# Spectral mix with a gated MLP: the first MLP block as seven products, with the first two products of three blocks ahead of the rest

## The chip, the cores and the metric

The kernel runs on one core of a Trainium2 chip. The time is device microseconds of one execution; three runs of the kernel before gave a median of 782.64 us (781.74 to 783.07). The core's engines work from queues of their own and wait for one another through semaphores: PE (TensorE, matrix multiply), DVE (VectorE), ACT (ScalarE), POOL (GpSimd) and SP (SyncE). SP and POOL issue nearly all DMAs here.

## The reference, cut to what matters

```python
x = A_x                                                    # 1 x 2048 x 512
g = sigmoid((x * gate_w).sum(-1, keepdims=True))
# FNet mixing: real part of a DFT over the hidden axis, then over the sequence
a = einsum("bsd,ed->bse", x, dft_hid_re)
b = einsum("bsd,ed->bse", x, dft_hid_im)
y = einsum("ts,bse->bte", dft_seq_re, a) - einsum("ts,bse->bte", dft_seq_im, b)
# gated MLP, F = 1792
gate = einsum("bsd,df->bsf", x, W_gate)
up = einsum("bsd,df->bsf", x, W_up)
h = gate * (gate > 0) * up
mlp = einsum("bsf,fd->bsd", h, W_down)
out = g * y + (1 - g) * mlp
```

## The kernel before, in words

All values are float32. Before a matmul each operand is split in two: `hi`, its value rounded to the matmul's input type (a cast), and `lo`, what is left (a subtraction on DVE). A product of two operands is then three matmuls, lo x hi, hi x lo and hi x hi (`PARTS`, L431), summed in PSUM. A cast and a subtraction stand behind every operand, so ACT and DVE feed PE.

Matrix products are made of 2 x 2 blocks, and nearly all of them with seven block products in place of eight, after Strassen and Winograd: some operands are sums of blocks (`x_sum`, `Weights.sum`), and the seven results are combined in PSUM by copying one bank's content into another before the next product is added on top ("seed" in `Block.evac`). The products are numbered 1 to 7 and run in the order 1, 5, 6, 2, 7, 3, 4 (`ORDER`, L25). Products 1 and 2 use the raw blocks of x and of the weights. Products 5, 6, 7, 3 and 4 use sums, or come after them.

The MLP's first stage (`Block`, L539) goes over blocks (c, q): c is one of seven pairs of 128-column groups of W_gate and W_up, and q one of two halves of the tokens. One product of a block is 12 matmuls of 128x512: two outputs i (gate, up), two halves k of the contraction and three parts. So a block of seven products takes 84 matmuls. One block is made otherwise: the first one, (0, 0), with eight plain products (`Direct`, L593), 96 matmuls, from weights laid out a second time in memory (`wf`). It loads x block 11 and its weights in small pieces, so that PE can begin after the first of them. Then come (1, 0), (2, 0), (2, 1), (1, 1) and the others in turn (`sequence`, L1294); block (0, 1) is last, behind the transform over the hidden axis. Behind the MLP's first stage come that transform, the MLP's second stage (`Down`) and the transform over the sequence (`Joint`, `Sequence`). Sums of the DFT matrices that the last stages need are made early, at times when DMA and DVE have room: `right_sums` (L931) loads four 512 KB blocks p, adds them on DVE and stores four sums to memory (`tb`), 18 times, at places from the table `SUMS` (L514).

What sets the order: the text of the kernel only gives each operation a key, which is a place on PE's own path counted in matmuls of 512 columns (0.2267 us each; called a number below). A planner in the kernel (`Plan`, L170) then plays the engines through with fixed costs for each kind of instruction, puts the operations of DVE and ACT in order of due time, and writes out one fixed order for each engine. For DMAs it has a model of its own (`Queues`, L126): a landing 2.4 us after the last byte, and 1.8 us more where another transfer is under way. The keys of prepared operands are in the table `AT` (L512). The weights of later blocks are asked for 66 numbers ahead of their block (`w_prep`, L501; 180 for the last block). Buffers come from 51 units of SBUF, PSUM has eight banks that are taken in turn.

Names in the lists below: `x011` is the loaded x block 11 of token half 0, `x012` and `x022` blocks 12 and 22, `xs5`, `xs6` sums; `xh7`, `xl7` the hi and lo of the x operand of product 7. `wr0`, `wr1` are loaded weights, `wr2`, `wr3` sums of them, `w1h`, `w1l` hi and lo made of `wr1`. In the profile's rows the numbers are left out (`xl`, `wr`), `xb11h` is `Direct`'s hi of x block 11, and `c` is a PSUM bank of the MLP's first stage. All instructions carry L123, the planner's one line of recording, so they are told apart by tile.

Before the first load has landed PE runs eight matmuls on a tile of ones (`warm_up`, L1249), all into one bank.

Of the kernel before, what the change touches and what calls it, by code (L numbers as in the profile page):

```python
# [125 lines left out]
class Queues:  # L126
# [3 lines left out]
    LANDING, BUSY = 2.4, 1.8  # L130
# [211 lines left out]
def kernel(ctx: ExitStack, tc, xP, xG, wf, wgu, wd, cr, ci, wri, gw, out):  # L342
# [129 lines left out]
    class Weights:  # L472
# [6 lines left out]
        def load(self, n):  # L479
            load(self.raw[n].all, wgu[self.c, n])  # L480
# [20 lines left out]
    def w_prep(w, key, ahead=66):  # L501
        for n in range(2):
            op(key - ahead + 6 * n, w.load, n)
        for m, n, k in ((None, 0, -40), (5, None, -36), (6, 2, -30), (7, 1, -12), (3, 3, 0)):
            if m:
                op(key + k, w.sum, m)
            if n is not None:
                op(key + k + 2, w.hi, n)
                op(key + k + 8, w.lo, n)


    AT = {'gate': (66, 52, 482), 'v': (-90, -80, -52, -36, -20, 6, 10, 38, 44), 'lw': (-246, -158, -138, -114, -110, -102), 'll': (-90, 22, 52, 96, 138, 174), 'l0': (-154, -58, -100, -8), 'l1': (-92, -120, -24, 44), 'z': (86,), 'J1': (80, 20, 78, 34, 94), 'J2': (172, 16, 38, 54, 98), 'J3': (136, 24, 56, 60, 64), 'hr': (36, 32, 45), 'rest': (62, 130)}  # L512

    SUMS = {(0, 3, 1): 1520, (0, 1, 1): 210, (1, 2, 0): 2452, (0, 1, 0): 685, (1, 5, 2): 260, (1, 1, 1): 687, (0, 2, 1): 955, (0, 3, 0): 1794, (1, 1, 0): 785, (1, 2, 1): 1000, (0, 2, 0): 377, (1, 4, 0): 444, (1, 3, 0): 655, (1, 3, 1): 800, (1, 5, 3): 1300, (1, 4, 2): 1632, (1, 5, 1): 1045, (1, 5, 0): 541}  # L514
# [24 lines left out]
    class Block:  # L539


        def __init__(self, q, w):
# [4 lines left out]
            for m in ORDER:  # L547
# [3 lines left out]
            h_out(q, w.c, self.h, plan.now + (8 if plan.now > 270 else 100))  # L551
# [11 lines left out]
        def evac(self, m, i):  # L563
# [7 lines left out]
            if m == 1:  # L571
# [19 lines left out]


    class Direct:  # L593
        def __init__(self):
            self.x = {b: [buf(f"xb{b}{x}", dtype=F32R) for x in "hl"] for b in ("11", "21", "12", "22")}

            self.raw = [buf(f"wf{d}", [2, 4, P]) for d in range(2)]
            self.w = [[buf(f"wf{d}{x}", [2, 4, P], F32R) for x in "hl"] for d in range(2)]
            self.g = [buf(f"dg{j}") for j in range(2)]
            self.h = [buf(f"h{d}") for d in range(2)]  # L600
            self.ps = {(f, j): Pair("c") for f in range(2) for j in range(2)}

            for d in range(2):
                for k in range(2):
                    for n in range(3):
                        for i in range(2):
                            pe(2, self.products, [(d, i, f, 0, k, n) for f in range(2)])
                            if d == k == 1 and n == 2:
                                for f in range(2):
                                    op(plan.now, self.evac, f, i, 0)  # L610
            for d in range(2):
                for i in range(2):
                    for f in range(2):
                        pe(6, self.products, [(d, i, f, 1, k, n) for k in range(2) for n in range(3)])
                        if d == 1:
                            op(plan.now, self.evac, f, i, 1)
            h_out(0, 0, self.h, plan.now + 200)
# [10 lines left out]
        def w_load(self, d, k, s=slice(0, 4)):  # L628
            load(self.raw[d][:, k, s], wf[d, :, k, s])

        def w_hi(self, d, k, s=slice(0, 4)):
            E().scalar.copy(self.w[d][0][:, k, s], self.raw[d][:, k, s])

        def w_lo(self, d, k):
            hi, lo = self.w[d]
# [784 lines left out]
```

## Time and profile before

| | us |
|---|---|
| median of three runs | 782.64 |
| profiled execution, its own time | 782.31 |
| its span, first to last instruction | 780.5 |
| PE busy | 774.1 |
| DVE busy | 706.8 |
| ACT busy | 467.4 |
| POOL busy | 119.6 |

The span is 1.8 us shorter than the execution's time; what lies around it is no instruction of the program. Busy time of PE says little about how near it is to its own pace, since matmuls overlap: one takes 389 ns from start to end, and the next starts 227 ns after it. So the distance from one start to the next is what to read, and where it grows PE has waited or its clock was held back.

### The profile page before, as it was taken

How to read it: one execution, taken by the hardware profiler on the slowest of the kernel's cores; microseconds unless marked ns; L12 is line 12 of the kernel's file. 1: busy time of each engine (PE TensorE's matmuls, PEld its weight loads, DVE VectorE, ACT ScalarE, POOL GpSimd, SP SyncE). 2: the span in 40 equal slices, each digit the busy share in tenths (PEclk: the TensorE clock that was granted, in tenths of full speed). 3: DMA queues.
4: the chain of work that ended last, by engine and by line, in shares of the span. 5: the costliest groups of instructions: out<-in, count | busy, mean ns of one | idle time of the engine just before them, and what ended most of it. 6: DMA issues, size and time to landing. Idle time of an engine off the chain costs nothing.

```text
span 780.5 us, 10195 instructions
## 1 busy us (share of the span) xinstructions
PE 774.1 (99%) x3416; PEld 640.3 (82%) x3416; DVE 706.8 (91%) x798; ACT 467.4 (60%) x649; POOL 119.6 (15%) x190
## 2 busy tenths in 40 slices
PE   8999999999999999999999999999999999999997
PEld 6888888888888888888888888888888888888886
DVE  7999898889797978899988579999999999999997
ACT  5654454444444744666565568955648897557672
POOL 0013422232223123212101000001020001010100
PEclk9999999999999999999999999999999999999999
DMA  8446999999989799999999998999989999999991
GB/s 317 181 166 239 381 409 411 379 418 420 418 339 419 303 361 416 418 388 416 376 410 380 406 397 256 371 407 410 309 319 310 375 408 348 335 336 364 314 361 55
DMA packets 78774, 274.12 MB, mean 351 GB/s; under 512 B 8960, under 2 KB 9728, under 8 KB 78720
## 3 DMA queue, kind: packets, MB, share of 16 engines
q1 hardware_dynamic: 52688, 179.47, 60.1%
q0 software_dynamic: 25888, 93.86, 33.6%
q8 instruction: 27, 0.44, 0.2%
q14 instruction: 27, 0.22, 0.1%
q10 hardware_dynamic: 144, 0.13, 0.0%
HBM read 183.76 MB, written 89.66 MB: 350 GB/s over the span
## 4 chain that ended last, share of the span: by engine, by line
PE 97%; DVE 2%; DMA 0%; issue 0%; ACT 0%; SPq 0%; ACTq 0%
PE z L123 39%; PE c L123 35%; PE a L123 10%; PE jB L123 3%; PE jA L123 3%; PE jX L123 2%; PE jD L123 2%; PE jG L123 1%; DVE jcl L123 1%; DVE jo L123 0%; PE jH L123 0%; DMA wf<-wf 0%; DVE jr L123 0%; ACT wf0h L123 0%; DVE wf0l L123 0%
## 5 line engine op out<-in xcount | busy, mean ns | idle before, releaser
L123 PE MATMUL z<-cl,lh 128*128 128x512 f32 x452 | 176.1, 390 | 0.0
L123 PE MATMUL z<-ch,lh 128*128 128x512 f32 x452 | 175.9, 389 | 0.0
L123 PE MATMUL z<-ch,ll 128*128 128x512 f32 x452 | 175.8, 389 | 0.0
L123 DVE TENSOR_TENSOR jcl<-jr,jch 128x1024 fp32r<-128x1024 f32 x84 | 99.5, 1216 | 0.9 <-issue 0.3
L123 PEld LDWEIGHTS z<-cl,lh 128*128 128x128 f32 x452 | 84.8, 188 | 17.9 <-DVE cl L123 0.6
L123 PEld LDWEIGHTS z<-ch,ll 128*128 128x128 f32 x452 | 84.8, 188 | 17.8
L123 PEld LDWEIGHTS z<-ch,lh 128*128 128x128 f32 x452 | 84.8, 188 | 17.7
L123 ACT CAST jch<-jr 128x1024 fp32r<-128x1024 f32 x84 | 85.4, 1053 | 16.8 <-PE z L123 5.8
L123 DVE TENSOR_TENSOR p<-p,p 128x1024 f32<-128x1024 f32 x72 | 86.8, 1219 | 5.6 <-DMA p<-ci 4.9
L123 ACT CAST ch<-r 128x1024 fp32r<-128x1024 f32 x64 | 65.9, 1051 | 36.7 <-DVE r L123 26.3
L123 ACT ACTIVATE c<-c 128x512 f32<-128x512 f32 x78 | 45.4, 583 | 69.0 <-PE c L123 58.1
L123 DVE TENSOR_TENSOR cl<-r,ch 128x1024 fp32r<-128x1024 f32 x64 | 76.9, 1219 | 0.6 <-ACT ch L123 0.4
L123 DVE TENSOR_TENSOR cl<-hr,ch 128x1024 fp32r<-128x1024 f32 (+1 forms) x56 | 60.0, 1087 | 12.7 <-ACT ch L123 8.6
L123 POOL DMA_DIRECT2D tb<-p x72 | 39.3, 546 | 171.6 <-DVE p L123 160.8
L123 ACT CAST ch<-hr 128x1024 fp32r<-128x1024 f32 (+1 forms) x56 | 51.6, 944 | 12.4 <-PE z L123 7.2
L123 PE MATMUL c<-xh,w2l 128*128 128x512 f32 x104 | 40.5, 389 | 0.0
L123 PE MATMUL c<-xl,w2h 128*128 128x512 f32 x104 | 40.5, 389 | 0.0
L123 PE MATMUL c<-xh,w2h 128*128 128x512 f32 x104 | 40.5, 389 | 0.0
L123 PE MATMUL c<-xh,w1l 128*128 128x512 f32 x104 | 40.5, 389 | 0.0
L123 PE MATMUL c<-xl,w1h 128*128 128x512 f32 x104 | 40.5, 389 | 0.0
L123 PE MATMUL c<-xh,w1h 128*128 128x512 f32 x104 | 40.5, 389 | 0.0
L123 ACT COPY a<-a 128x512 f32<-128x512 f32 x40 | 23.1, 579 | 25.9 <-PE a L123 21.0
(229 smaller groups left out, 1636.5 us busy)
## 6 DMA issues: line engine op xcount, KB each, us to landing
tb<-p POOLq DMA_DIRECT2D x72, 512.0 KB, 11.1
p<-ci SPq DMA_DIRECT2D x48, 512.0 KB, 9.3
jr<-tb SPq DMA_DIRECT2D x48, 512.0 KB, 7.7
hr<-hd SPq DMA_DIRECT2D x42, 512.0 KB, 8.6
hd<-hs POOLq DMA_DIRECT2D x28, 512.0 KB, 10.6
ad<-a POOLq DMA_DIRECT2D x28, 512.0 KB, 8.9
p<-cr SPq DMA_DIRECT2D x24, 512.0 KB, 8.4
r<-cr SPq DMA_DIRECT2D x24, 512.0 KB, 12.0
```

What stands on the lines that cost most here:

```text
L123: getattr(getattr(nc, self.engine), self.name)(*map(ap, self.a), **{k: ap(x) for k, x in self.k.items()})
```

## The change

Block (0, 0) is made as the others are, with seven products, and `Direct` and its second copy of the weights are gone. The three blocks c = 0, 1, 2 of token half 0 begin together: product 1 of block 0, product 1 of block 1, product 2 of block 0, product 1 of block 2, product 2 of block 1, product 2 of block 2, half of the contraction after half. The result of product 1 is copied from PSUM to an SBUF buffer `p` by ACT (two copies for each block). Then each block goes on with products 5, 6, 7, 3, 4, after two ACT copies have seeded a bank from `p`.

The first loads are now pieces of the usual weight arrays: x block 11 and the weights of product 1 of blocks 0 and 1, then x block 21 and the weights of product 2. The planner's DMA model adds its 1.8 us only behind its first 10 us. The eight warm-up matmuls go to four banks in turn. The keys of the tables `AT` and `SUMS` are other numbers, among them the places of the sums, where one line shows the whole table:

```diff
-    LANDING, BUSY = 2.4, 1.8
+    LANDING, BUSY, EARLY = 2.4, 1.8, 10
...
-            s.end = t + self.LANDING + (self.BUSY if busy else 0)
+            s.end = t + self.LANDING + (self.BUSY if busy and t > self.EARLY else 0)
...
-    def hi_of(t):
-        E().scalar.copy(t[0].all, t[2].all)
-
-    def lo_of(t):
-        E().vector.tensor_sub(t[1].all, t[2].all, f32(t[0].all))
+    def hi_of(t, k=slice(0, 2), copy=None):
+        (copy or E().scalar.copy)(t[0][:, k], t[2][:, k])
+
+    def lo_of(t, k=slice(0, 2)):
+        E().vector.tensor_sub(t[1][:, k], t[2][:, k], f32(t[0][:, k]))
...
-        def load(self, n):
-            load(self.raw[n].all, wgu[self.c, n])
+        def load(self, n, f=slice(0, 4)):
+            load(self.raw[n][:, f], wgu[self.c, n, :, f])
...
-        def part(self, n, x):
-            return self.w[n][x].all if n < 3 else self.w3[:, 2 * x:2 * x + 2]
-
-        def hi(self, n):
-            E().scalar.copy(self.part(n, 0), self.raw[n].all)
-
-        def lo(self, n):
-            E().vector.tensor_sub(self.part(n, 1), self.raw[n].all, f32(self.part(n, 0)))
+        def part(self, n, x, f):
+            return self.w[n][x][:, f] if n < 3 else self.w3[:, 2 * x:2 * x + 2]
+
+        def hi(self, n, f=slice(0, 4)):
+            E().scalar.copy(self.part(n, 0, f), self.raw[n][:, f])
+
+        def lo(self, n, f=slice(0, 4)):
+            E().vector.tensor_sub(self.part(n, 1, f), self.raw[n][:, f], f32(self.part(n, 0, f)))
...
-    SUMS = {(0, 3, 1): 1520, (0, 1, 1): 210, (1, 2, 0): 2452, (0, 1, 0): 685, (1, 5, 2): 260, (1, 1, 1): 687, (0, 2, 1): 955, (0, 3, 0): 1794, (1, 1, 0): 785, (1, 2, 1): 1000, (0, 2, 0): 377, (1, 4, 0): 444, (1, 3, 0): 655, (1, 3, 1): 800, (1, 5, 3): 1300, (1, 4, 2): 1632, (1, 5, 1): 1045, (1, 5, 0): 541}
+    SUMS = {(0, 3, 1): 1550, (0, 1, 1): 100, (1, 2, 0): 457, (0, 1, 0): 955, (1, 5, 2): 2362, (1, 1, 1): 657, (0, 2, 1): 1632, (0, 3, 0): 1794, (1, 1, 0): 775, (1, 2, 1): 1000, (0, 2, 0): 260, (1, 4, 0): 444, (1, 3, 0): 655, (1, 3, 1): 800, (1, 5, 3): 1300, (1, 4, 2): 685, (1, 5, 1): 1035, (1, 5, 0): 511}
...
-            for m in ORDER:
+            self.part = None
+
+        def run(self, order=ORDER):
+            for m in order:
                 for i in range(2):
                     pe(6, self.product, m, i)
                     op(plan.now, self.evac, m, i)
-            h_out(q, w.c, self.h, plan.now + (8 if plan.now > 270 else 100))
+            h_out(self.q, self.w.c, self.h, plan.now + (8 if plan.now > 270 else 100))
+
+        def begin(self, m):
+            self.part = self.part or buf("p")
+            for k in range(2):
+                for n in range(3):
+                    pe(2, self.pieces, m, k, n)
+            for i in range(2):
+                op(plan.now, self.evac, m, i)
+
+        def pieces(self, m, k, n):
+            ps, (a, b) = self.ps["A"], PARTS[2 - n]
+            if m == 1 and k == n == 0:
+                ps.new()
+            for i in range(2):
+                mm(ps[i], self.w.of(m, i)[a][:, k], X[self.q, m][b][:, k], start=m == 1 and k == n == 0, stop=k == 1 and n == 2)
+
+        def resume(self, key):
+            def seed():
+                self.ps["X"].new()
+                for i in range(2):
+                    E().scalar.copy(self.ps["X"][i], self.part[:, i])
+
+            op(key, seed)
+            self.run(ORDER[1:3] + ORDER[4:])
...
-            if m == 1:
+            if m == 1 and self.part:
+                e.scalar.copy(self.part[:, i], p["A"][i])
+            elif m == 1:
...
-    class Direct:
...
-        def products(self, all):
-            for d, i, f, j, k, n in all:
-                first = d == k == n == 0
-                if first and i == 0:
-                    self.ps[f, j].new()
-                a, b = PARTS[2 - n]
-                mm(self.ps[f, j][i], self.w[d][a][:, k, 2 * i + f], self.x["12"[d] + "12"[j]][b][:, k],
-                   start=first, stop=d == k == 1 and n == 2)
...
-    warm, wp = buf("warm", [P], F32R), Pair("warm")
+    warm, wp = buf("warm", [P], F32R), [Pair("warm") for _ in range(2)]
 
     def warm_up():
         E().vector.memset(f32(warm.all), 1.0)
-        wp.new()
+        for p in wp:
+            p.new()
         for n in range(WARM):
-            mm(wp[0], warm.all, warm.all.unsqueeze(1).to_broadcast([P, N // P, P]), start=n == 0, stop=n == WARM - 1)
+            mm(wp[n % 4 // 2][n % 2], warm.all, warm.all.unsqueeze(1).to_broadcast([P, N // P, P]), start=n < 4, stop=n >= WARM - 4)
 
     NP = KF // 2
-    w1, direct = Weights(1), Direct()
+    w0, w1, w2 = Weights(0), Weights(1), Weights(2)
     for b in ("11", "21", "12", "22"):
         x_piece(0, b)
+    for m in ORDER:
+        x_raw(0, m)
     op(-100, warm_up)
     halves = [slice(0, 1), slice(1, 2)]
     pairs = [slice(0, 2), slice(2, 4)]
-    for d, b in ((0, "11"), (1, "21")):
-        for k in range(2):
-            op(-99, x_load, 0, b, halves[k])
-            for s in pairs if d == 0 else [slice(0, 4)]:
-                op(-99, direct.w_load, d, k, s)
-    for f, *a in ((x_load, 0, "12"), (x_load, 0, "22"), (w1.load, 0), (w1.load, 1), (lambda: load(gwt[:], gw),)):
+    for b, f in (("11", pairs[0]), ("21", pairs[1])):
+        for k, w in zip(halves, (w0, w1)):
+            op(-99, x_load, 0, b, k)
+            op(-99, w.load, 0, f)
+    for f, *a in ((x_load, 0, "12"), (w2.load, 0), (w0.load, 1), (x_load, 0, "22"), (w1.load, 1), (w2.load, 1), (lambda: load(gwt[:], gw),)):
         op(-98, f, *a)
-    for m, b in ((1, "11"), (2, "21"), (3, "22")):
-        X[0, m] = *direct.x[b], piece[0, b]
-    for d, b in ((0, "11"), (1, "21")):
-        for k in range(2):
-            op(-90, direct.x_split, b, halves[k], plan.vector.tensor_copy if d == 0 else None)
-            if d == 0:
-                for s in pairs:
-                    op(-90, direct.w_hi, d, k, s)
-                op(-90, direct.w_lo, d, k)
-            else:
-                op(-90, direct.w_split, d, k)
+    for m, f in ((1, pairs[0]), (2, pairs[1])):
+        for k, w in zip(halves, (w0, w1)):
+            op(-90, hi_of, X[0, m], k, plan.vector.tensor_copy if m == 1 else None)
+            op(-90, lo_of, X[0, m], k)
+            op(-90, w.hi, 0, f)
+            op(-90, w.lo, 0, f)
     op(-85, lambda: E().vector.memset(gs.all, 0.0))
-    op(-80, direct.x_split, "12")
-    op(-80, direct.x_split, "22")
-    for m in (4, 5, 6, 7):
-        x_raw(0, m)
-    for k, f, *a in ((20, w1.hi, 0), (20, w1.lo, 0), (30, w1.sum, 5), (32, w1.sum, 6), (34, w1.hi, 2), (36, w1.lo, 2),
-                     (50, w1.sum, 7), (52, w1.hi, 1), (54, w1.lo, 1), (60, w1.sum, 3), (62, w1.hi, 3), (64, w1.lo, 3)):
-        op(k, f, *a)
-    for n, m in enumerate((5, 6, 7, 4)):
+    op(-20, w2.hi, 0)
+    op(-20, w2.lo, 0)
+    for m, key in zip((5, 6, 7, 3, 4), AT["open"]):
         for f, *a in ((x_sum, 0, m), (hi_of, X[0, m]), (lo_of, X[0, m])):
-            op(40 + 10 * n, f, *a)
+            op(key, f, *a)
+    for w, key in zip((w0, w1, w2), AT["w0"]):
+        for k, f, *a in ((3, w.sum, 5), (5, w.sum, 6), (6, w.hi, 2), (7, w.lo, 2), (22, w.sum, 7), (23, w.hi, 1), (24, w.lo, 1),
+                        (32, w.sum, 3), (33, w.hi, 3, pairs[0]), (34, w.lo, 3, pairs[0])):
+            op(key + k, f, *a)
+    opening = [Block(0, w) for w in (w0, w1, w2)]
+    for n, m in ((0, 1), (1, 1), (0, 2), (2, 1), (1, 2), (2, 2)):
+        opening[n].begin(m)
+    for b in opening:
+        b.resume(plan.now - 8)
 
...
-    sequence = [(1, 0), (2, 0), (2, 1), (1, 1)]
+    sequence = [(2, 1), (1, 1)]
-    ws = {1: w1}
+    ws = {1: w1, 2: w2}
...
-            if c == 2 and q == 0:
+            if (c, q) == (2, 1):
                 for b in ("22", "11", "12", "21"):
                     x_piece(1, b)
-                    op(plan.now - 100, x_load, 1, b)
+                    op(plan.now + AT["x"][0], x_load, 1, b)
                 for n, m in enumerate(ORDER):
-                    x_prep(1, m, plan.now - 46 + 27 * n)
-            Block(q, ws[c])
...
-        "wf": laid(first),
```

The order of the instructions shows it at three places. First the queue of SP at the program's start, where loads are issued in turn. Before:

```order
L123 DMA x011_78<-xP 128x512
L123 DMA wf0_82<-wf 128x256 x2
L123 DMA x011_78<-xP 128x512
L123 DMA wf0_82<-wf 128x256 x2
L123 DMA x021_95<-xP 128x512
L123 DMA wf1_97<-wf 128x512
L123 DMA x021_95<-xP 128x512
L123 DMA wf1_97<-wf 128x512
L123 DMA x012_106<-xP 128x1024
L123 DMA x022_111<-xP 128x1024
L123 DMA wr0_118<-wgu 128x1024
L123 DMA wr1_127<-wgu 128x1024
```

And in the changed kernel:

```order
L123 DMA x011_78<-xP 128x512
L123 DMA wr0_82<-wgu 128x512
L123 DMA x011_78<-xP 128x512
L123 DMA wr0_93<-wgu 128x512
L123 DMA x021_97<-xP 128x512
L123 DMA wr0_82<-wgu 128x512
L123 DMA x021_97<-xP 128x512
L123 DMA wr0_93<-wgu 128x512
L123 DMA x012_106<-xP 128x1024
L123 DMA wr0_110<-wgu 128x1024
L123 DMA wr1_116<-wgu 128x1024
L123 DMA x022_124<-xP 128x1024
```

Four loads of 128 KB have become two of 256 KB, so eight loads stand ahead of block 12 of x in place of ten. Weights of block 2 (`wr0_110`) and the second weights of block 0 (`wr1_116`) stand ahead of x block 22, which was ahead of all weights of the second block.

Second, DVE's first instructions behind the fill of the warm-up tile. Before:

```order
L123 TENSOR_TENSOR wf0l_104<-wf0_82,wf0h_99 128x512
L123 CAST xb11h_108<-x011_78 128x512
L123 TENSOR_TENSOR xb11l_113<-x011_78,xb11h_108 128x512
L123 TENSOR_TENSOR wf0l_104<-wf0_82,wf0h_99 128x512
L123 CAST xb11h_108<-x011_78 128x512
```

And in the changed kernel:

```order
L123 CAST xh1_102<-x011_78 128x512
L123 TENSOR_TENSOR xl1_104<-x011_78,xh1_102 128x512
L123 TENSOR_TENSOR w0l_112<-wr0_82,w0h_108 128x512
L123 CAST xh1_102<-x011_78 128x512
L123 TENSOR_TENSOR xl1_104<-x011_78,xh1_102 128x512
```

The cast of x, which the first matmul needs, no longer stands behind the lo of the weights.

Third, DVE's order from the sums for block 0's later products up to the lo of the weights of its product 7 (`w1l_324`). It is the end of the piece from the fourteenth to the twenty-ninth instruction:

```order
L123 TENSOR_TENSOR xs6_237<-x022_124,xs5_171 128x1024
L123 TENSOR_TENSOR x021_97<-x021_97,xs6_237 128x1024
L123 TENSOR_TENSOR w2l_256<-wr2_214,w2h_229 128x1024
L123 TENSOR_TENSOR h0_265<-g_222,c_118 128x512
L123 TENSOR_TENSOR xl4_271<-x021_97,xh4_260 128x1024
L123 TENSOR_TENSOR xl6_278<-xs6_237,xh6_252 128x1024
L123 TENSOR_TENSOR x012_106<-x022_124,x012_106 128x1024
L123 TENSOR_TENSOR wr1_116<-wr0_82,wr1_116 128x512
L123 TENSOR_TENSOR wr3_303<-wr0_82,wr2_214 128x512
L123 TENSOR_TENSOR h0_308<-g_269,c_154 128x512
L123 TENSOR_TENSOR xl7_315<-x012_106,xh7_301 128x1024
L123 TENSOR_TENSOR w1l_324<-wr1_116,w1h_311 128x1024
```

Ahead of these twelve stand, from the fourteenth on, `w0l_202` (the lo of block 2's first weights, 128x1024), two sums `wr2_214` (128x512) and `xl5_226` (128x1024). In the kernel before, the lo of product 7's weights was instruction 26 (`w1l_287`), and belonged to the second block.

More of the change, by code (lines that the diff above doesn't have):

```diff
@@ L341, with kernel @@
 @with_exitstack
-def kernel(ctx: ExitStack, tc, xP, xG, wf, wgu, wd, cr, ci, wri, gw, out):
+def kernel(ctx: ExitStack, tc, xP, xG, wgu, wd, cr, ci, wri, gw, out):
     nc = tc.nc
@@ L1303, in blocks @@
                 w_prep(ws.setdefault(c, Weights(c)), plan.now, 66 if c else 180)
-            if c == 2 and q == 0:
+            if (c, q) == (2, 1):
                 for b in ("22", "11", "12", "21"):
                     x_piece(1, b)
-                    op(plan.now - 100, x_load, 1, b)
+                    op(plan.now + AT["x"][0], x_load, 1, b)
                 for n, m in enumerate(ORDER):
-                    x_prep(1, m, plan.now - 46 + 27 * n)
-            Block(q, ws[c])
+                    x_prep(1, m, plan.now + AT["x"][1 + n])
+            Block(q, ws[c]).run()
     blocks(sequence)
@@ L1398 @@
     wgu = np.stack([blocks(wg), blocks(wu)], axis=3)
-    first = wgu[0][:, [[0, 3], [1, 2]]].transpose(1, 0, 4, 3, 2, 5).reshape(2, P, 2, 4, P)
     wgu = wgu.reshape(KF // 2, P, 2, 4, 2, P).transpose(0, 2, 1, 3, 4, 5)
```

49 lines of the change are left out of this document (4 added, 45 removed).

## The prediction

> **What bounds the kernel now.** I read the page's busy times and chain first, then the waits of PE, then the chain in order of time, and last the first 80 us instruction by instruction.
>
> ```profile
> PE 774.1 (99%) x3416; PEld 640.3 (82%) x3416; DVE 706.8 (91%) x798; ACT 467.4 (60%) x649; POOL 119.6 (15%) x190
> ...
> PE 97%; DVE 2%; DMA 0%; issue 0%; ACT 0%; SPq 0%; ACTq 0%
> ```
>
> ```profile
> PE c L123 <- DVE xb11h L123: 1.1, 1, 1.1
> PE warm L123 <- DVE warm L123: 1.1, 1, 1.1
> PE jH L123 <- DVE jcl L123: 0.5, 1, 0.5
> ```
>
> ```profile
> 1.19 2.77 DMA wf<-wf
> 3.96 0.02 issue
> 3.98 0.77 ACT wf0h L123 x2
> 4.75 0.02 issue
> 4.77 0.69 DVE wf0l L123
> 5.46 0.35 DVE xb11h L123
> 5.81 0.14 issue
> 5.95 252.59 PE c L123 x1104
> ...
> 334.70 19.04 PE c L123 x84
> ```
>
> PE carries 97% of the chain and waits three times in 780 us, of which only the first real matmul's wait and the one near the end count. 84 matmuls take 19.04 us, 226.7 ns each. So PE's count of matmuls is worth its full price wherever DVE can feed it. DVE is 91% busy: it is the engine that could become the bound.
>
> The beginning has a pace of its own:
>
> ```profile
> 1.06 3.78 PE L123 MATMUL warm<-warm 128*128 128x512 f32 x8 [1.06 <-DVE warm L123]
> 5.95 2.05 PE L123 MATMUL c<-xb11h,wf0h 128*128 128x512 f32 x4 [1.11 <-DVE xb11h L123]
> 7.79 1.91 PE L123 MATMUL c<-xb11l,wf0h 128*128 128x512 f32 x4
> 9.50 1.52 PE L123 MATMUL c<-xb11h,wf0l 128*128 128x512 f32 x4
> 10.86 1.07 PE L123 MATMUL c<-xb11h,wf0h 128*128 128x512 f32 x4
> 11.77 1.07 PE L123 MATMUL c<-xb11l,wf0h 128*128 128x512 f32 x4
> ```
>
> From 7.79 to 9.50 four starts take 1.71 us, 427 ns each; from 10.86 to 11.77, 0.91 us, 227 each. PE runs at half pace until about 10.35 us, though the clock column of the profile says 1.00 there.
>
> **The change part by part.** Removed: 96 matmuls of `Direct`, for 84 of a block. 12 x 0.2267 = **2.72 us** of PE. The real matmuls fall from 3408 to 3396. I compare the two kernels at places with equally many matmuls to come. The rows of before at two such places, its 109th and 314th real matmul:
>
> ```profile
> 32.62 0.39 PE L123 MATMUL c<-xh,w2l 128*128 128x512 f32 x1
> ...
> 79.09 0.39 PE L123 MATMUL c<-xl,w1h 128*128 128x512 f32 x1
> ```
>
> They answer to the changed kernel's 97th and 302nd: the first matmul of block 0's product 7 (72 + 24 ahead of it), which wants `w1l`; and the second of block (2, 1)'s product 7 (252 + 49 ahead), which wants `xl7` of token half 1.
>
> *PE by itself.* The first matmul now waits for the hi of a 256 KB weight load, no longer for x behind `wf0l`. Before, the same 512 KB were there when the second cast of `wf` began: two of 0.40 end at 4.75, so 4.35.
>
> ```profile
> L123 ACT CAST wf0h<-wf x4: 402/404/407, 4.0 to 6.3; 128x256 fp32r<-128x256 f32 x4
> ...
> 8.36 0.62 ACT L123 CAST xb21h<-x 128x512 fp32r<-128x512 f32 x1 [1.67 <-DMA x<-xP]
> ```
>
> A cast of 512 columns takes 0.62: 4.97, and 0.14 to PE's start as in the chain: 5.1 in place of 5.95. If half pace still ends at 10.35, 12 matmuls run till then and the 97th starts at 10.35 + 84 x 0.2267 = 29.4; if it ends 4.4 us behind the first start as before, at 29.0. Against 32.62 PE alone saves 3.2 to 3.6.
>
> A rule speaks to this: the Trainium skill (TensorE: Matmul & The Clock Gate, "Part 1: The HAM clock gate") has PE at half clock until it was busy through one free-running window of about 3.4 us. The rows agree in the pace, 427 against 227 ns. By that rule a window ended at 10.35 and one at 6.94, and with PE now busy almost without a break from 1.06 on the gate could open at 6.94, with the 97th at 27.8 and 4.8 saved by PE alone.
>
> *DVE.* It now has in the first 30 us the preparation of three blocks' first weights. From its fourteenth instruction on (the lo of block 2's weights) nothing in its order is short of data for long, so I add up its own time. Periods and the start come from these rows:
>
> ```profile
> 12.10 1.05 ACT L123 CAST xb12h<-x 128x1024 fp32r<-128x1024 f32 x1 [0.68 <-DMA x<-xP]
> 13.37 1.06 ACT L123 CAST xb22h<-x 128x1024 fp32r<-128x1024 f32 x1 [0.22 <-DMA x<-xP]
> ```
>
> ```profile
> 14.46 1.23 DVE L123 TENSOR_TENSOR xb22l<-x,xb22h 128x1024 fp32r<-128x1024 f32 x1
> 15.60 1.22 DVE L123 TENSOR_TENSOR xs<-x,xs 128x1024 f32<-128x1024 f32 x1
> 16.74 1.22 DVE L123 TENSOR_TENSOR w0l<-wr,w0h 128x1024 fp32r<-128x1024 f32 x1
> 17.87 0.69 DVE L123 TENSOR_TENSOR wr<-wr 128x512 f32<-128x512 f32 x1
> 18.59 0.69 DVE L123 TENSOR_TENSOR wr<-wr,wr 128x512 f32<-128x512 f32 x1
> 19.20 0.68 DVE L123 TENSOR_TENSOR h<-dg,c 128x512 f32<-128x512 f32 x1
> ```
>
> 1024 columns take 1.14 from start to start, 512 take 0.60, and one that reads its forerunner's result 0.1 more (17.87 to 18.59). The load of block 2's weights completes the first 3072 KB, as x block 22 did before, whose cast began at 13.37. With the same landing the cast ends and DVE starts at 14.46. Instructions 14 to 28 are nine of 1024 columns and six of 512: 10.26 + 3.60 + 0.2; `w1l` itself takes 1.22: ready at 29.74, and PE's 97th starts at 29.9. That is **later than PE by itself** (29.0 to 29.4): PE will wait 0.5 to 0.9 us there, the new stall of this change. Up to `xl7` of half 1, instructions 14 to 86 are 30 of 1024 and 43 of 512: 34.2 + 25.8 + 0.8 for eight that follow their own input, + 1.22: 76.5, and PE's 302nd starts at 76.65. PE itself would be there 205 matmuls behind the 97th, 29.9 + 46.5 = 76.4: a second wait of 0.3. So saved against 79.09: **2.4**.
>
> The landing is the open term. Two issues less stand ahead on SP, 0.43 us each (the median of the first row below), so at most 0.9 earlier; the bytes are the same, and the DMA engines were nearly full:
>
> ```profile
> L123 SPq DMA_DIRECT2D wf<-wf x6: 422/432/438, 1.2 to 5.0; - x6
> ```
>
> ```profile
> 6.00:7.00 1.00, 1.00 (x3) 0.81 (x4) 0.81 (x2) 0.68 (x2) 0.00 (x0) 1.00 0.80 211
> 7.00:8.00 1.00, 1.00 (x4) 0.81 (x3) 0.96 (x3) 0.00 (x0) 0.00 (x0) 1.00 0.83 248
> ```
>
> At a DMA share of 0.80 to 0.83 (last but one column) some of the 0.9 can be had. I take 0.3, nearer to none since bytes set it; bounds 0 and 0.9. Saved then 2.7, bounds 2.4 and 3.3; PE alone caps it at about 3.2 with half pace to 10.35 (10.35 + 289 x 0.2267 = 75.9 at the 302nd).
>
> *ACT* gets six copies into `p`, six seeds and the seven-product block's evacuations. They stand in the same queue as the casts, and each waits for PE's product; a cast behind one is late when PE is. Up to block 2's weights the queue has one pair of copies and one of seeds; product 1 of block 0 is done near 10.4, before those weights land. Cost taken: 0; if such a wait shows up on DVE it counts in full, as a rival below.
>
> *Moved sums.* By number 1100 (250 us) 13 sums are asked for in both tables, but three stand at 444, 457 and 511 in place of 444 and 541, and two rather than three before 400. DMA is full there:
>
> ```profile
> 75.00:150.00 75.00, 75.00 (x332) 62.12 (x331) 67.75 (x91) 35.62 (x59) 24.18 (x38) 1.00 1.01 392
> 150.00:210.00 60.00, 60.00 (x266) 49.67 (x265) 49.70 (x62) 25.83 (x44) 18.37 (x31) 1.00 1.02 417
> 210.00:240.00 30.00, 30.00 (x134) 24.84 (x133) 28.05 (x36) 13.37 (x22) 7.60 (x13) 1.00 0.94 368
> ...
> wr<-wgu SPq DMA_DIRECT2D x8, 512.0 KB, 9.1
> ```
>
> A sum is eight transfers of 512 KB, 4.19 MB, 10.1 us at 417 GB/s. What covers it: weights are asked for 66 numbers (15.0 us) ahead and land 9.1 us after issue, 5.9 to spare, less 2.3 for a cast and a lo; and 0.94 in the last window shows the backlog worked off. Taken as 0.
>
> *The end* is unchanged code, and its one wait, on `jcl`, stays.
>
> The sum: 782.31 (profiled time, 1.8 around its span of 780.5) - 2.7 = 779.6. The median of the runs shown is 0.3 above that execution, so I forecast **779.9**.
>
> **The rivals.**
> 1. *Loads land early.* With the landing 0.9 sooner DVE's chain gives 3.3, PE alone 3.2 to 3.6: 779.2. For: fewer, larger loads. Against: bytes. By the clock rule of the Trainium skill above, PE would not cap it, and 779.0 would be in reach.
> 2. *DVE's chain slips.* It is busy without a break for 62 us, so a lost microsecond anywhere, by a cast behind a copy of `p` or a slow load, goes to PE in full. Losing 1 to 2 us leaves 0.7 to 1.7: 781.0 to 782.0, middle 781.5. For: before, DVE lost 0.5 us at 21 to a cast. Against: the orders put the copies behind the casts that matter.
> 3. *The crowded sums hold back weights.* If the third sum between 444 and 511 is not absorbed, a block's weights land 10.1 us late, 3.6 are to spare, and PE waits 6.5: 782.64 - 2.7 + 6.5 = 786.4, slower. It decides once the lateness passes 3.6 + 2.7 = 6.3 us. For: shares of 1.01 and 1.02. Against: 45 to 75 us and 210 to 240 have room, and the sums are elsewhere less dense.
>
> **How the numbers follow.** My forecast, 2.2 to 3.1 saved, gets 0.62; rival 1 0.15, rival 2 0.16, rival 3 0.07. A difference under 0.2%, 1.6 us, can't be told from no change. Faster: forecast, rival 1 and a small part of rival 2, 0.79; the same: most of rival 2, 0.14; slower 0.07. The range takes in rival 1 and rival 2: 778.9 to 781.9.
>
> **What would show it.** PE's first real matmul near 5.1 us; half pace ending by 10.4; a wait of PE on DVE `w1l` near 29 us (0.2 to 0.9, about 2 if half pace ends at 7) and on `xl` near 76 us (about 0.3); DVE without a gap between 14.5 and 76; no wait of PE between 80 and 530. I am wrong if PE waits elsewhere in the MLP's first stage, if the landing of block 2's weights moves by over 1 us, or if ACT's copies show as what DVE waited for.

## The result, and the profile after

| | before | after |
|---|---|---|
| median, us (5 runs each, side by side) | 782.64 | 779.03 |
| lowest to highest | 780.36 to 783.07 | 778.97 to 779.9 |
| profiled execution, its own time | 782.31 | 779.1 |
| its span | 780.5 | 777.3 |
| real matmuls | 3408 | 3396 |

The ratio is 0.9962, its 95% interval 0.9947 to 0.9978: 0.38% faster, 3.6 us by the medians and 3.2 us between the two profiled executions. The forecast was 779.9, within 778.9 to 781.9. So the measured median lies inside the range but close to its lower end, and 3.6 us by the medians is more than the 2.2 to 3.1 that the forecast itself was meant to cover.

The first thing to look at in the new profile is the chain that ended last, by engine: PE had 97% of it before.

```profile
PE 88%; DVE 9%; DMA 1%; issue 1%; SPq 1%; ACT 0%; DVEq 0%; ACTq 0%
```

Most of DVE's 9% stands in one piece, from 14.08 to 76.48 us. The same chain in order of time (start, duration, what), with most of the DVE steps between left out:

```profile
5.42 7.55 DMA wr<-wgu
12.99 1.06 ACT w0h L123
14.08 1.23 DVE w0l L123
...
28.24 1.14 DVE w1l L123
29.97 1.14 DVE xl L123
...
75.21 1.23 DVE xl L123
76.48 3.70 PE c L123 x15
```

Read it from the end: the matmul at 76.48 was released by a subtraction on DVE, that one by DVE's row before it, and so back to 14.08, where DVE began on block 2's weights as soon as they had landed (12.97) and were cast. Between the two times PE doesn't stand on the chain at all. What PE waited for says it in a few numbers (in total, times, longest):

```profile
PE warm L123 <- DVE warm L123: 1.1, 1, 1.1
PE c L123 <- ACT w0h L123: 0.5, 1, 0.5
PE jH L123 <- DVE jcl L123: 0.5, 1, 0.5
PE c L123 <- DVE xl L123: 0.2, 1, 0.2
```

And how full DVE is meanwhile, busy 62.05 of 62.35 us (fourth column of times) in the first window here, while PE has no gap in the second:

```profile
14.08:76.43 62.35, 62.09 (x273) 50.79 (x271) 62.05 (x75) 42.08 (x66) 7.34 (x13) 1.00 0.52 203
80.00:530.00 450.00, 450.00 (x1986) 372.63 (x1985) 399.10 (x477) 258.19 (x378) 92.04 (x148) 1.00 1.00 392
```

The two places at which the prediction compared the kernels are the 97th and the 302nd matmul. In PE's timeline of after:

```profile
29.07 0.39 PE L123 MATMUL c<-xh,w2h 128*128 128x512 f32 x1
29.52 0.47 PE L123 MATMUL c<-xh,w1l 128*128 128x512 f32 x1
...
75.85 0.39 PE L123 MATMUL c<-xh,w1l 128*128 128x512 f32 x1
76.48 0.50 PE L123 MATMUL c<-xl,w1h 128*128 128x512 f32 x1 [0.25 <-DVE xl L123]
```

A start distance of 0.45 at the first and of 0.63 at the second, where 0.227 is PE's own pace: waits of 0.22 and 0.40 us. Against 32.62 and 79.09 before, after is 3.10 us ahead at the first place and 2.61 at the second. The last matmul starts at 773.71 where it was 776.48, 2.77 ahead, and from there to the end of the span it is 3.6 instead of 4.0 us.

Two parts of the change were not run apart from the rest: the other keys of `AT`, and the four banks of the warm-up. Of the warm-up the profiles say that its eight matmuls stand at the same place in both (from 1.06 us, 3.78 us long).

### The profile page after: what moved, and what is told of

Same layout as the page of the kernel before. It is cut to its first block, busy times and chain, and to the rows that moved or that the text cites. A ratio compares the mean times of both kernels' runs of the same rounds, so it can differ in the third digit from the quotient of the medians.

```text
span 777.3 us, 10201 instructions
## 1 busy us (share of the span) xinstructions
PE 771.6 (99%) x3404; PEld 638.2 (82%) x3404; DVE 711.3 (92%) x807; ACT 475.8 (61%) x662; POOL 120.0 (15%) x190
## 4 chain that ended last, share of the span: by engine, by line
PE 88%; DVE 9%; DMA 1%; issue 1%; SPq 1%; ACT 0%; DVEq 0%; ACTq 0%
PE z L123 40%; PE c L123 26%; PE a L123 10%; PE jB L123 4%; PE jA L123 3%; PE jX L123 2%; PE jD L123 2%; PE jG L123 1%; DVE xl L123 1%; DVE h L123 1%; DVE p L123 1%; DMA wr<-wgu 1%; DVE wr L123 1%; DVE jcl L123 1%; DVE x L123 1%
## 5 line engine op out<-in xcount | busy, mean ns | idle before, releaser
L123 PE MATMUL c<-xl,w1h 128*128 128x512 f32 x112 | 43.7, 390 | 0.2 <-DVE xl L123 0.2
L123 PE MATMUL c<-xh,w1l 128*128 128x512 f32 x112 | 43.7, 390 | 0.1
L123 PE MATMUL a<-vl,xh 128*128 128x512 f32 x112 | 43.6, 389 | 0.0
L123 PE MATMUL a<-vh,xl 128*128 128x512 f32 x112 | 43.6, 389 | 0.0
L123 PE MATMUL c<-xh,w1h 128*128 128x512 f32 x112 | 43.6, 389 | 0.0
L123 PE MATMUL c<-xh,w2l 128*128 128x512 f32 x112 | 43.6, 389 | 0.0
L123 PE MATMUL c<-xl,w2h 128*128 128x512 f32 x112 | 43.6, 389 | 0.0
```

Source lines behind the costliest of these rows:

```text
L123: getattr(getattr(nc, self.engine), self.name)(*map(ap, self.a), **{k: ap(x) for k, x in self.k.items()})
```

## The experiments

All changes are made to the changed kernel, except where the kernel before is named. "Before" in the last two columns is the kernel before on the same chip, in between; chips differ from call to call.

| run | median, us (range, runs) | before | ratio, 95% interval |
|---|---|---|---|
| e1_skip_early | 778.66 (778.59 to 779.27, 5) | 781.92 | 0.9965, 0.9952 to 0.9978 |
| e2_skip_late | 776.11 (776.0 to 776.35, 4) | 781.92 | 0.9931, 0.9915 to 0.9948 |
| e3_warm10 | 779.26 (778.86 to 779.47, 7) | 781.92 | 0.9966, 0.9955 to 0.9977 |
| e4_old_sums | 783.17 (781.49 to 784.83, 10) | 781.92 | 1.0020, 1.0009 to 1.0031 |
| e5_pool_sum | 789.36 (788.55 to 790.54, 4) | 782.46 | 1.0096, 1.0070 to 1.0122 |
| e6_pool_sums2 | 794.27 (793.56 to 794.75, 4) | 782.46 | 1.0160, 1.0131 to 1.0188 |
| e7_before_warm10 | 780.61 (779.87 to 782.57, 10) | 782.46 | 0.9986, 0.9971 to 1.0002 |
| e8_early0 | 779.08 (778.3 to 780.59, 9) | 782.46 | 0.9965, 0.9951 to 0.9978 |
| e9_after_again | 779.44 (778.68 to 780.23, 12) | 781.38 | 0.9975, 0.9965 to 0.9984 |
| e10_sum_later | 783.64 (782.28 to 785.83, 10) | 781.38 | 1.0029, 1.0016 to 1.0042 |
| e11_before_new_sums | 783.97 (782.2 to 785.56, 10) | 782.22 | 1.0023, 1.0010 to 1.0037 |

**Twelve matmuls less, inside and behind the stretch that DVE sets.** Both runs leave the matmuls of one product 4 out of the program after the orders are made, so that every other queue keeps its order; block (0, 0) is inside the first 76 us, block (3, 0) begins behind them.

```diff
+                    plan.steps[-1].ghost = (self.w.c, self.q, m) == (0, 0, 4)    # e2: (3, 0, 4)
...
     def run(self, nc):
+        if getattr(self, "ghost", False):
+            return
```

> The changed kernel without the 12 matmuls of product 4 of the first block (0, 0); every other instruction and every order stays, and block 22 of that block's h is not computed. Theory A (DVE sets the pace from 14 to 76 us, so PE's own count is worth nothing there): PE is 2.7 us ahead from about 35 us on, waits for DVE instead (about 3.1 us in all near 76 us, in place of 0.5), its 302nd place, the second matmul of product 7 of block (2, 1), starts at 76.5 as before, and the span stays at 777.3 +- 0.3. Rival B (12 matmuls are worth 2.72 us wherever they stand, as the prediction's first term has it): that matmul starts at 73.8 and the span is 774.6.

> The changed kernel without the 12 matmuls of product 4 of block (3, 0), which comes behind 76 us; every other instruction and every order stays, and one block of that block's h is not computed. Theory A and rival B agree: PE waits nowhere there, so the span falls by 2.7 to 774.6. A third view, that DVE or DMA sets the pace behind 76 us too, has the span at 777.3.

PE's waits in the first of the two profiles:

```profile
PE c L126 <- DVE w1l L126: 1.1, 1, 1.1
PE c L126 <- DVE w L126: 1.1, 1, 1.1
...
PE c L126 <- ACT g L126: 0.5, 1, 0.5
...
PE c L126 <- DVE xl L126: 0.4, 1, 0.4
```

(The edit adds lines to the kernel, so that the planner's line is L126 here and in e5.) The first of these waits ends at the 97th matmul, at 29.40, and isn't due to the edit, for product 4 of block 0 comes behind the 97th; it is due to an early full pace, as in e3 below. The other three stand behind it; after has only the last of them, with 0.2. The 302nd place:

```profile
76.14 0.50 PE L126 MATMUL c<-xl,w1h 128*128 128x512 f32 x1 [0.37 <-DVE xl L126]
```

From the 97th place to this one it is 46.74 us, and 46.96 in after. So of the 2.72 us that PE no longer works 2.5 turn up as waits on DVE and ACT. The 302nd place is 0.34 earlier in all, 0.13 of it because DVE started on block 2's weights at 13.95 and not at 14.08. The span is 776.9, 0.4 less, 0.1 outside what theory A allowed. The same twelve matmuls taken out behind 76 us give a span of 774.3, 3.0 less: 0.24 of it is there at the 302nd matmul already (76.24), and 2.7 come behind it. Inside the stretch PE's work has next to no price, behind it the full one.

**The clock's start.** Ten warm-up matmuls in place of eight (`WARM = 10`), once in the changed kernel, once in the kernel before.

> The changed kernel with ten warm-up matmuls in place of eight, which fill the pause of 0.5 us ahead of PE's first real matmul. Clock: if half pace ends at the end of a free-running window (about 6.9 us), it ends 2.5 to 3 us sooner than the 9.7 of the changed kernel; if it ends about 4.4 us behind the first real matmul whatever is before it, it stays at 9.7 to 9.9. Theory A: whichever it is, PE's 97th matmul (first of product 7 of block 0) still starts at 29.5, behind w1l, and the span stays at 777.3 +- 0.3; with the early clock the wait there grows from 0.2 to about 2. Rival B: the early clock is worth 1.2 to 1.5 us of span.

> The kernel before with ten warm-up matmuls instead of eight. Theory A says that before, PE waits for nothing from its first real matmul on, so the moment at which the half pace ends passes into the time whole: each us that it ends earlier saves 1 - 227/427 = 0.47 us. With the end at t, the 314th matmul should start at 79.09 - 0.47 x (10.35 - t): near 77.0 if the full pace is there from the first real matmul (5.95), and the span 2.1 below 780.5, 778.4. That would also be the spread of the kernel before from 780.4 to 783.7. Rival F: VectorE holds the kernel before too, at 29 or 77 us, and the 314th matmul stays near 79 whatever the clock does.

In both profiles PE ran at full pace from its first real matmul on, sooner than either moment that was expected for e3. The kernel before:

```profile
1.06 4.28 PE L123 MATMUL warm<-warm 128*128 128x512 f32 x10 [1.06 <-DVE warm L123]
6.01 1.17 PE L123 MATMUL c<-xb11h,wf0h 128*128 128x512 f32 x4 [0.68 <-DVE xb11h L123]
...
77.08 0.39 PE L123 MATMUL c<-xl,w1h 128*128 128x512 f32 x1
```

Four matmuls take 1.17 us where they took 2.05, and its 314th stands at 77.08, where 77.0 was expected, with the span at 778.1 (778.4 expected): the kernel before has its time from PE alone, and gains 2.0 us at that place when the half pace ends early. Rival F is out. In the changed kernel the same cause moved nothing: the 97th matmul came at 29.58 after a wait of 1.2 us on `w1l`, the 302nd at 76.55, and the span is 777.3 again.

The number of warm-up matmuls can't be credited with it. With eight of them, in other profiles of this study, the full pace was there by the first real matmul too (e1, at 5.46 us, and e2, e4, e5, e10), or came at 6.5 (e8) and 7.1 us (e9). The ten runs of e7 still spread over 779.87 to 782.57, the kernel before on that chip over 779.83 to 783.99, and the interval of their ratio takes in no change.

**The changed kernel once more.**

> The changed kernel once more, for the spread of its times and a second profile beside runs of the kernel before on the same chip. Theory A: VectorE paces PE up to 76 us, so the moment of the full pace, which moved the kernel before by 2.4 us of span between two profiles (10.35 us: 780.5; 5.0 us: 778.1), does not reach the end: the 302nd matmul starts between 76.0 and 76.6, the span is 777.3 within 0.4 wherever the half pace ends, and the times lie closer together than those of the kernel before. Rival F: the times spread as widely as those of the kernel before, and the 302nd matmul moves by 1 us or more with the clock.

PE's timeline at the two places:

```profile
28.45 0.39 PE L123 MATMUL c<-xh,w2h 128*128 128x512 f32 x1
29.98 0.47 PE L123 MATMUL c<-xh,w1l 128*128 128x512 f32 x1 [1.14 <-DVE w1l L123]
...
76.97 0.50 PE L123 MATMUL c<-xl,w1h 128*128 128x512 f32 x1 [0.24 <-DVE xl L123]
```

The 302nd matmul is 0.4 later than the highest value expected, and the span of 777.8 is 0.1 outside what was allowed, though the half pace ended 2.6 us earlier than in the first profile of after. The cause is DVE's start: block 2's weights landed at 13.42 in place of 12.97, and DVE began on them at 14.53, 0.45 later. From that start to the 302nd matmul it is 62.44 us here, 62.40 in the first profile, 62.41 in e3 and 62.19 in e1. So the moment of the full pace doesn't reach the end, and the landing does; no run sets the landing, so this rests on how it varied by itself. The times lie within 1.6 us, those of the kernel before on that chip within 3.7. The gain there is 1.9 us by the medians, less than the 3.6 first seen; the two intervals of the ratio overlap.

**The order of the first casts.**

```diff
-    LANDING, BUSY, EARLY = 2.4, 1.8, 10
+    LANDING, BUSY, EARLY = 2.4, 1.8, 0
```

> The changed kernel with the planner's assumption on late first landings put back (all landings 1.8 us late while other queues are busy, not only those after 10 us), so that VectorE's rows around the second casts stand in another order. Theory A: VectorE's sum of work up to the operand of the 302nd matmul is the same, 62 us, so that the 302nd starts near 76.5 again and the time is 779.0, within 0.3. Rival G: the order of the first casts is what the gain comes from, and without it a wait of 1 us or more stands near 15 to 30 us and reaches the end: 780 or more.

779.08, and the 302nd matmul at 75.94, 61.9 us behind DVE's start at 14.00. DVE's rows ahead of `w1l` are fewer by one, so the 97th matmul came at 28.60. G is out: the first casts may be planned with or without the lateness.

**The table of the right sums.** The old table in the changed kernel, then the new table in the kernel before. The keys that differ in the first 100 us, and where the sum (1, 5, 2) goes:

```diff
-    SUMS = {..., (0, 1, 1): 100, (0, 2, 0): 260, (1, 5, 2): 2362, ...}
+    SUMS = {..., (0, 1, 1): 210, (0, 2, 0): 377, (1, 5, 2): 260, ...}    # e4; e11 the other way
```

> The changed kernel with the table SUMS of the kernel before (the places of the 18 right sums); all else, the seven-product opening too, as changed. Prediction's view (moved sums cost and bring nothing): span 777.3 +- 0.5. Theory C (the old places put the sums' adds on DVE at 48 and 59 us ahead of token half 1's operands, and DVE has no room left there): PE waits about 2 us for an operand of block (2, 1) near 76 to 80 us, and the span is 779 to 780, so that the new opening without the moved sums gains about a fifth of what the whole change did.

> The kernel before with the changed kernel's table of right sums, the other half of the run with the old table in the changed kernel. Theory A: before, PE waits for nothing up to 314 matmuls, so a better place of the sums has nothing to remove: the same time within 0.3 and, with the half pace ending at t, a span of 780.5 - 0.47 x (10.35 - t). Rival J: the table is made for the changed order, and in the old one its earlier adds (keys 100 and 260 in place of 210 and 377) push VectorE's operands behind PE, with waits of 1 us or more before 80 us: 783 or more. Rival K: the table alone is what brought the gain, and the kernel before gets 2.7 faster with it: 779.

In e4 PE waited here:

```profile
78.70 0.39 PE L123 MATMUL c<-xh,w 128*128 128x512 f32 x1
81.82 0.50 PE L123 MATMUL c<-xl,w 128*128 128x512 f32 x1 [2.73 <-DVE xl L123]
```

and DVE's timeline shows what stood ahead of that `xl`:

```profile
73.42 4.87 DVE L123 TENSOR_TENSOR p<-p,p 128x1024 f32<-128x1024 f32 x4
78.21 1.22 DVE L123 TENSOR_TENSOR xl<-x,xh 128x1024 fp32r<-128x1024 f32 x1
79.34 0.69 DVE L123 TENSOR_TENSOR hs<-h 128x512 f32<-128x512 f32 x1
79.94 0.68 DVE L123 TENSOR_TENSOR hs<-h,h 128x512 f32<-128x512 f32 x1
80.55 1.22 DVE L123 TENSOR_TENSOR xl<-x,xh 128x1024 fp32r<-128x1024 f32 x1
```

All four adds of a sum in a row, just ahead of the operands of token half 1; it is the sum (1, 5, 2), which the new table asks for at 2362. The two `xl` that e4 has at 78.21 and 80.55 end at 79.8 in after. The span is 779.9, within theory C's 779 to 780, though the adds stand later than it had them. The 302nd matmul starts at 76.20 here, a little earlier than in after: what the table sets shows behind the place up to which the prediction added up DVE's rows. In seven of the ten runs the mean granted clock was also only 0.996 to 0.998, and those took 782.9 to 784.8, the other three 781.5 to 782.3. By the medians the change with the old table is 1.25 us slower than the kernel before.

In the kernel before the new table does nothing up to 79.12, the 314th matmul (79.09 before). Its cost stands where no theory had put it, in the last stage:

```profile
554.94 0.39 PE L123 MATMUL z<-ch,ll 128*128 128x512 f32 x1
556.97 0.50 PE L123 MATMUL z<-cl,lh 128*128 128x512 f32 x1 [1.65 <-DVE cl L123]
```

```profile
553.30 2.48 DVE L123 TENSOR_TENSOR p<-p,p 128x1024 f32<-128x1024 f32 x2
555.70 1.22 DVE L123 TENSOR_TENSOR cl<-r,ch 128x1024 fp32r<-128x1024 f32 x1
```

Again adds of a sum ahead of an operand. Theory A and rival K fail. J has the time right (783 or more) but not the place: no wait stands before 80 us. The table fits one order of the program and costs 1.75 us by the medians in the other.

**Taking load off DVE, three tries.** Two put adds of right sums on GpSimd, one asks for a sum later.

```diff
+        elif engine == "gpsimd":
+            self.work = 0.2 + n * 2.2e-3
+            self.hold = self.work
...
-    def combine(o, a, b, sign):
-        (plan.vector.tensor_add if sign > 0 else plan.vector.tensor_sub)(o, a, b)
+    ON_POOL = ((0, 1, 1),)    # e6: ((0, 1, 1), (0, 2, 0))
+
+    def combine(o, a, b, sign, on_pool=False):
+        e = plan.gpsimd if on_pool else plan.vector
+        (e.tensor_add if sign > 0 else e.tensor_sub)(o, a, b)
```

> The four adds of right sum (0, 1, 1), which stand on VectorE at 32.95, 36.42, 38.16 and 41.03 us of the changed kernel's profile, run on GpSimd; nothing else is meant to change. Theory A (VectorE's backlog from 14 to 76 us is what PE waits for): 4 x 1.14 = 4.6 us leave VectorE between the 97th and the 302nd matmul, the wait of 0.4 us at 76 us goes, the one near 29 us stays (0.2 to 1.2, as the clock opens late or early), and the 302nd matmul starts 205 x 0.2267 = 46.47 us behind the 97th, near 76.0 instead of 76.5: about 778.5 us, 0.5 less than the changed kernel. Rival C (the two engines get in each other's way): VectorE's 128x1024 instructions take more than 1.22 us while GpSimd adds, the wait at 76 stays, and the time is 779 or more. Rival D (the sums come late and something of the main stage waits): PE waits on a DMA later.

> As the run before, with the four adds of right sum (0, 2, 0) on GpSimd too, three of which stand on VectorE at 67 to 71 us. Theory A: the wait at 76 us had gone already, and the wait near 29 us is older than both sums, so nothing further comes: 778.5 again, within 0.2. Rival E (VectorE is behind right through the main stage and every add taken from it is worth its 1.14 us): 4.6 us less, 774.

The planner put the four adds at 21 to 34 us. POOL's and DVE's timelines of e5 there:

```profile
21.25 2.40 POOL L126 TENSOR_TENSOR p<-p,p 128x1024 f32<-128x1024 f32 x1 [20.80 <-DMA p<-cr]
...
24.70 2.40 POOL L126 TENSOR_TENSOR p<-p,p 128x1024 f32<-128x1024 f32 x1
...
28.02 2.39 POOL L126 TENSOR_TENSOR p<-p,p 128x1024 f32<-128x1024 f32 x1
...
31.30 2.43 POOL L126 TENSOR_TENSOR p<-p,p 128x1024 f32<-128x1024 f32 x1
```

```profile
19.93 1.22 DVE L126 TENSOR_TENSOR w2l<-wr,w2h 128x1024 fp32r<-128x1024 f32 x1
...
21.66 3.07 DVE L126 TENSOR_TENSOR xl<-x,xh 128x1024 fp32r<-128x1024 f32 x1
24.66 3.53 DVE L126 TENSOR_TENSOR xl<-xs,xh 128x1024 fp32r<-128x1024 f32 x1
28.11 3.38 DVE L126 TENSOR_TENSOR x<-x,x 128x1024 f32<-128x1024 f32 x1
31.42 3.46 DVE L126 TENSOR_TENSOR wr<-wr,wr 128x512 f32<-128x512 f32 x2
```

Rival C, and much worse than it said. Each add on GpSimd holds up one DVE row by 1.9 to 2.3 us: the five instructions take 13.4 us where the same shapes took 5.0 in after (3 x 1.22 and 1.29). DVE loses 8.5 us to be spared 4.6 later, the 97th matmul comes at 37.89 in place of 29.52, and the span is 786.8. (PE's wait of 5.40 us there is put down to an ACT copy, which comes just behind DVE's late rows.) Behind the 97th matmul theory A holds, but it doesn't help: from the 97th to the 302nd matmul (86.25) it is 48.36 us, which is PE's own 46.47 and 1.9 lost to half pace behind the long wait. With two sums there (e6) the span is 791.8, which neither of its two views had.

> The changed kernel with right sum (0, 1, 1) due at matmul 330 instead of 100: its four adds (4.6 us) stay on VectorE, but behind the operand of the 302nd matmul. Theory A: the wait at 76 us goes, the 302nd matmul starts 205 x 0.2267 = 46.47 us behind the 97th, at 76.0 or up to 0.5 earlier, and the time is 778.5 if VectorE has room for the adds behind it. Rival H: VectorE and the DMA queues have no room between 76 and 160 us, where they are busy for 97% and more: a new wait of 0.5 us or more stands there and the time is 779 or more.

```diff
-    SUMS = {..., (0, 1, 1): 100, ...}
+    SUMS = {..., (0, 1, 1): 330, ...}
```

The first half of theory A held, the 302nd matmul started at 76.06 and 46.70 us behind the 97th, and so did the wait that rival H named: PE waited 2.8 us behind it, on an `xl` as in e4.

```profile
78.55 0.39 PE L123 MATMUL c<-xh,w 128*128 128x512 f32 x1
81.74 0.50 PE L123 MATMUL c<-xl,w 128*128 128x512 f32 x1 [2.80 <-DVE xl L123]
```

DVE's timeline shows what stood ahead of that `xl`:

```profile
76.10 1.23 DVE L123 TENSOR_TENSOR xl<-x,xh 128x1024 fp32r<-128x1024 f32 x1 [1.38 <-PE c L123]
...
79.17 1.22 DVE L123 TENSOR_TENSOR p<-p,p 128x1024 f32<-128x1024 f32 x1
80.46 1.23 DVE L123 TENSOR_TENSOR xl<-x,xh 128x1024 fp32r<-128x1024 f32 x1
```

It was not a lack of room: DVE stood idle for 1.38 us ahead of the `xl` at 76.10, which the profile puts down to PE. Then three rows of 512 columns and an add of the moved sum ran before the `xl` that PE wanted; in after the last two `xl` stand in a row and end at 79.8. None of the three tries beats the changed kernel.

## Why the prediction was right, point by point

- *Removed matmuls.* Twelve fewer, and 2.72 us was the right size for what came of it (2.77 at the last matmul). But e1 shows that this agreement is luck and no proof of the step: in the stretch up to 76 us twelve matmuls are worth 0.2 us, 0.34 with the earlier landing of that run. The gain there is the difference between two limits, PE's own work before and DVE's backlog after, as the prediction had worked it out in its DVE part.
- *PE by itself.* First real matmul 5.37, not 5.1: the weights whose cast it waits for landed at 4.68, not by 4.35. The half pace ended near 9.7 (9.5 or 10.35 were taken), and without its wait the 97th would have started at 29.3 (29.0 to 29.4). In e9 the half pace ended at 7.1, and the wait there was 1.3 us (1.53 from start to start, less 0.23), where the prediction had about 2 for that case. DVE came when it said (97th at 29.98, forecast 29.9); it was PE that would have been there at 28.7 and not at 27.8: it started 0.1 later, the half pace ended 0.2 later, and small delays on the way add up to 0.6.
- *DVE.* The step that carries the result, and it held. From DVE's start on block 2's weights to the 302nd matmul 62.4 us, forecast 62.2; waits of 0.22 and 0.40, forecast 0.2 to 0.9 and 0.3. The landing came 0.4 earlier than in the kernel before, forecast 0.3 with bounds 0 and 0.9. So 2.6 saved at the 302nd matmul, forecast 2.7. In ten profiles of the changed kernel and its variants with the same loads that landing came between 12.70 and 13.42: this much is left to it.
- *ACT.* As forecast: DVE was never without work for long behind a copy of `p`, with 0.3 us idle in the 62.35 us.
- *Moved sums, taken as 0.* Wrong as a term. In the changed kernel the new table is worth 3.9 us by the medians (783.17 against 779.26 of e3 on the same chip; 2.6 between the profiled spans), in the kernel before it costs 1.75. I had looked for its price in DMA bandwidth beyond 100 us (rival 3); it lies in which rows of DVE stand ahead of an operand. The prediction added up DVE's rows only as far as the 302nd matmul, and the waits of e4 and e10 stand behind it. That the new table fits the changed order made the term come out near 0 in this sum; nothing in the working had shown that it would, so this is luck.
- *The end.* Between the 302nd and the last matmul 0.16 us less (2.61 becomes 2.77 ahead), and about 0.4 less from there to the end of the span; 0 was forecast for both. They make up the difference between 2.6 and 3.2. The 0.16 is less than two profiles of one kernel differ by there (697.4 and 697.0 us in the two of the kernel before). The 0.4 goes with the change, 4.0 us in every profile of the order before and 3.6 in every profile of the changed one; its cause stays open.
- *A fixed start.* The one assumption that the prediction didn't name as one is that the profiled execution before, with the half pace up to 10.35 us, stands for the others. With an early full pace the kernel before has a span of 778.1, and the gain is 0.3 to 0.8 us (against 777.8 and 777.3 after). By the medians it is 3.6 us in the first comparison and 1.9 in e9's, on another chip, on either side of the forecast's 2.2 to 3.1. How much of that is the half pace, and how much the chip, no run separates. That the median came out inside the range is in part luck.
- *Rivals.* None took place as described. The median of 779.03 is the time of the first (779.2, or 779.0 with the early clock) and not its cause: the landing came 0.4 earlier and not 0.9, the half pace ended near 9.7 in the profile, and in e9 and e3, where it ended sooner, DVE held PE at the 97th matmul all the same. The second, DVE slipping by 1 to 2 us, is what e4 and e10 become, with 3 us.

## What to carry to other kernels

When a saving on the busiest engine lies in a stretch where another engine has a backlog, add up that engine's rows from its first landing to the last operand it owes; the sum, here 62 us and right within 0.3, says when the stretch ends, and the saved instructions don't. A table of places for background work belongs to one order of the program and is to be tuned again with it: the same table was worth 3.9 us in one order and cost 1.75 in the other, by the medians. Before a gain below 0.5% is read from one profile, look at where the half pace at the start ended in it.

## What the runs showed of the hardware

*When the full pace comes differs from run to run.* Near 9.7, 7.1 and 6.5 us, and before 5.5 us in others, all with eight warm-up matmuls from 1.06 us on. The Trainium skill (TensorE: Matmul & The Clock Gate, "Part 1: The HAM clock gate") has the clock released by a free-running window of about 3.4 us, so that the moment varies with the start. The runs agree that it varies, but 9.7 us (10.35 in the kernel before) is 8.6 (9.3) us behind the first warm-up matmul, more than two such windows, with a pause of 0.5 (1.1) us ahead of the first real matmul; no run shows what the pause does. Where PE alone sets the time, the moment reaches the end (2.0 us at the 314th matmul and 2.4 us of span between two profiles of the kernel before), and the rule was of more use for the spread than for the one value.

*A short wait can bring the half pace back.* PE's timeline of e5, around a wait of 2.29 us:

```profile
25.57 0.39 PE L126 MATMUL c<-xh,w2l 128*128 128x512 f32 x1
28.24 0.80 PE L126 MATMUL c<-xl,w2h 128*128 128x512 f32 x1 [2.29 <-DVE xl L126]
28.84 0.63 PE L126 MATMUL c<-xh,w2h 128*128 128x512 f32 x1
29.27 0.63 PE L126 MATMUL c<-xh,w2l 128*128 128x512 f32 x1
...
31.40 0.40 PE L126 MATMUL c<-xh,w2h 128*128 128x512 f32 x1
```

The seven starts behind 28.24 take 3.16 us in place of 1.59, so 1.6 us are lost in addition to the wait. In e10 the half pace followed 1.3 us behind a wait of 2.80, in e4's profile not at all behind one of 2.73. The same section has the clock fall back after an idle window of about 3.4 us; here less than one was enough, sometimes. So a wait of 2 to 3 us cost up to 1.6 us on top in these profiles, and e5's wait of 5.40 us 1.9.

*An add on GpSimd holds DVE up.* In e5 a DVE row with two operands in SBUF got longer by nearly the whole of GpSimd's 2.40 us. That is what the Trainium skill says (SBUF — State Buffer, "SBUF: two separate sides"): the two engines share a pair of ports, and the first to take it holds it for its whole instruction. So an add moved there cost DVE 1.9 to 2.3 us in e5, where it spared 1.14.
